# A chunked-attention and gated-MLP kernel: 64-row attention tiles without padding, weight factors made during attention, one gated block taken from PSUM

## The chip, the cores and the metric

The kernel runs on one core of one Trainium2 chip. The metric is the device time of one execution in microseconds, lower is better. A time that is given for a kernel is the median of its runs; a profile shows one execution, whose own time is given beside it.

## The reference

Attention in chunks of 32 tokens, each of which sees 16 tokens to its left, 8 to its right and 8 memory tokens, feeds a gated MLP whose gate mixes the tokens of a sequence:

```python
# B, H, S, D = 4, 8, 768, 64; 8 memory tokens; d_model 512, d_ff 1024
for c in range(S // 32):
    k_full = concat([mem_k, k[l_start:r_end]]); v_full = concat([mem_v, v[l_start:r_end]])
    s = q_c @ k_full.T / sqrt(D)
    a = exp(s - max(s)); a = a / (sum(a) + 1e-9)
    attn[c] = a @ v_full
x = attn as (B, S, 512)
h = relu(x @ w_in); u, v = halves of h
v_n = (v - mean) / sqrt(var + 1e-6)
v_s = einsum('ts,bsd->btd', w_spatial, v_n) + b_spatial
out = (u * v_s) @ w_out
```

## The kernel before

**A recorded order.** Every piece of work is recorded with `op(...)` (line 40): its engine, a guessed duration, what it reads and writes, a rank. `Plan.order` (line 64) plays all pieces through once with those guesses, always taking the piece that can start first and, among equals, the one with the lower rank; the program is written out in that order, so each engine runs its pieces strictly in the planner's sequence. Buffers come from rings (`sizes`, line 188), and a piece can also be held back until a slot of its ring is free. All loads and stores but three go through SyncE's queue (`transfer`, line 255), which never has more than a set number of MB outstanding (`window`, 1.5 MB).

**Attention.** A unit `i` is 128 tokens (four chunks of 32) of all eight heads; there are 24 units, six to a batch. The heads lie in four pairs `t`; in a pair, head `r` takes the partitions `r*64` to `r*64+63`. For the scores, `prep` (line 372, ScalarE) copies the keys of a unit into `kmain`, whose slots are 32 keys and 8 memory keys wide. `kmain` is block-diagonal: it has a column block for each of the two heads, and in the block of one head the other head's 64 partitions are zero. So one matmul with all 128 rows, 32 stationary columns of `q` and 2 x 64 moving columns gives the scores of both heads of a pair for one chunk. The values stand in `vmain` in the same manner. The zeros are written once, at the start (lines 239 to 243), and loads, copies and the spreading of the memory rows (`spread_mem`, `spread_keys`) only touch the other parts.

`burst(i)` (line 392) holds the matmuls on TensorE: 16 for the scores of unit `i` (part "s"), 16 for the product with the values of unit `i-1` (part "a"). For the first units the parts are two pieces of work, later they stand together. The target `sx` is a tile of two PSUM banks: all scores in one, all products in the other. Each of these fp32 matmuls appears in the profile as two records, so a part is 32. `softmax` (VectorE and ScalarE), two transposes (`flip`: `pt` for the probabilities, `xt` for the result) and the split of the result into a high and a low fp32r half (`x`) follow.

**MLP, first half.** `ffn_v` and `ffn_u` (lines 549, 588) multiply `x` and `w_in`, each product in three passes (high by high, low by high, high by low). They fill TensorE between the steps of attention as soon as three units of a half sequence are there. The normalised `v` and the `u` go out to DRAM and come back in the second half. `w_in` and `w_out` arrive as 64-bit floats and are taken apart by `from_f64` (line 813: two passes of ScalarE, two of VectorE, an addition on GpSimd); then `right_hand` (line 866) makes the seven right-hand factors.

**Second half.** `spatial(b)` and `ffn_o(b)` (lines 718, 767) are matrix products by a scheme of seven block products (`product`, line 637): p1 to p7 of sums of quarters. VectorE makes the sums (`sm`, line 651) and the low halves (`op`, line 667), ScalarE the high halves (`op`, line 664). Results of `spatial` are collected by a ScalarE copy (`take`, line 731) and a VectorE addition (`join`, line 737) and multiplied with `u` on GpSimd (`gate`, line 745). The seven factors of `w_spatial` come in three pairs of row blocks (`w_sp_pair`, line 913): two are made during attention into `wsp`, the third waits until attention has ended ("attended") and goes to a tile `wsp_end` in memory that attention has given back. `w_out`'s conversion is ordered behind a factor of that third pair (line 903), its factors behind the last matmul of the MLP's first half.

Of the kernel before, what the change touches and what calls it, by code (L numbers as in the profile page):

```python
# [18 lines left out]
CH = 32  # L19
# [6 lines left out]
class Plan:  # L26
# [13 lines left out]
    def op(self, eng, us, fn, r=(), w=(), rank=0.0, mb=0.0, tail=0.0, after=None, alone=False, drag=1.0):  # L40
# [20 lines left out]
        self.ops.append((eng, us, fn, deps, rank, mb, tail, held, begun, alone, drag))  # L61
        return n

    def order(self):
# [9 lines left out]
        lone = 0.0  # L74
# [7 lines left out]
        while len(out) < len(ops):  # L82
# [21 lines left out]
            _, us, _, _, _, mb, tail, held, _, alone, drag = ops[n]  # L104
# [5 lines left out]
            if alone:  # L110
                lone = t + us
            if mb:
# [30 lines left out]
def tile_chunked_attention_gmlp(  # L143
# [44 lines left out]
    sizes = {"f": 3, "sx": 1, "pt": 2, "xt": 1, "y": 5, "st": 8, "big": 4, "uo": 2, "x": 2, "vm": 3,  # L188
             "q": 2, "k": 2, "kT": 2, "p": 1, "xs": 1, "pT": 1, "vr": 2, "op": 4, "sm": 2, "ug": 6, "ot": 11}
    plan = Plan(sizes, {"f", "y", "st", "big", "ot"}, rate=0.30, landing=2.5, lat=0.06, window=1.5, early=(9.0, 4.0))  # L190
# [21 lines left out]
    wsp = const.tile([P, 7, 2, HU - 1, HT], F32R, name="wsp")  # L212
# [110 lines left out]
    def v_of(i):  # L323
        o = (i % NV) * UC
        return vmain[:, :, :, o:o + UC]

    def load_v(i, seq=True, second="SP"):
        b, c0 = i // UB, (i % UB) * UC
        n = UC
        for r in range(2):  # L330
            v4 = v_of(i)[:, :, r].rearrange("p t c d -> p t (c d)")
# [27 lines left out]
    def spread_mem(i, eng, rank):  # L359
        b, o = i // UB, (i % NV) * UC  # L360
        for r in range(2):
            rows = slice(r * D + CH, r * D + SLOT)

            def spread(rows=rows, r=r):
                to, of = vmain[rows, :, r, o:o + UC], memv[rows, b].unsqueeze(2).broadcast_to([M, T, UC, D])
# [6 lines left out]
    def prep(i, rank):  # L372
        for r in range(2):
            rows = slice(r * D, (r + 1) * D)

            def keys(r=r, rows=rows):
                nc.scalar.copy(kmain[i % NK][rows, :, r, :, 0:CH], k_of(i)[rows].rearrange("p t (c s) -> p t c s", s=CH))  # L377
            n = T * (UC + 1) * CH
            op("ACT", act(n), keys, r=qk_keys(i, "k"),
               w=[("kmain", i % NK, r)], rank=rank)  # L380

    def spread_keys(i, rank):
        b = i // UB

        def spread():
            for r in range(2):
                rows = slice(r * D, (r + 1) * D)
# [4 lines left out]
    def burst(i, rank, split=False):  # L392
# [680 lines left out]
```

## Time and profile before

| what | value |
|---|---|
| time, median of 3 runs | 396.16 us (395.98 to 396.25) |
| profiled execution's own time | 395.85 us |
| HBM read, written in it | 45.49 MB, 18.87 MB |
| packets of the main DMA queue | 46900, 64.25 MB, 53.5% of 16 engines' span |
| busiest groups of GpSimd | `ug<-st,ug` 43.8 us, `vmain<-memv` 23.8 us |

The profile gives times from the start of its span. PE is TensorE (PEld its weight loads), DVE VectorE, ACT ScalarE, POOL GpSimd, SP SyncE. In a group `out<-in xN`, out and in are tile names of the program. In a view by windows, each row is a stretch of the span with the busy time of each engine and the number of its instructions, then the granted clock of TensorE, the share of DMA and GB/s.

### The profile page before, as it was taken

The numbers are of one execution on the slowest core, as the hardware profiler recorded it, in microseconds if no ns is written. First come the engines' busy times: TensorE is split into PE (matmuls) and PEld (weight loads), VectorE is DVE, ScalarE is ACT, GpSimd is POOL, SyncE is SP. The second block draws the span as 40 slices with busy tenths as digits, with TensorE's granted clock in tenths as the row PEclk, the third lists the DMA queues.
The fourth block names the chain that finished last, engine by engine and source line by source line (L and its number), as shares of the span: only waits on it lengthen the run. The fifth ranks groups of instructions, "written<-read, shape, count | busy, mean of one in ns | idle before, by whom it ended". The sixth has DMA issues, their size and how long they took to land.

```text
span 394.1 us, 8707 instructions
## 1 busy us (share of the span) xinstructions
PE 368.4 (93%) x3428; PEld 335.0 (85%) x3428; DVE 281.0 (71%) x465; ACT 210.2 (53%) x368; POOL 157.5 (40%) x161
## 2 busy tenths in 40 slices
PE   1659899999999999999999998899999999999996
PEld 1437688898898988988889898799999999999996
DVE  7975965756856558866575499978956794788594
ACT  4765646575456557464434475438434734473361
POOL 8433762193621177601012968770226033403520
PEclk9999999999999999999999999999999999999999
DMA  8998567676575683786603768403640562040014
GB/s 231 309 232 210 129 202 230 183 251 185 182 219 160 235 221 112 211 223 206 187 29 136 257 237 278 136 25 121 210 153 0 162 233 89 0 175 27 2 40 161
DMA packets 47356, 64.93 MB, mean 165 GB/s; under 512 B 4434, under 2 KB 38866, under 8 KB 47316
## 3 DMA queue, kind: packets, MB, share of 16 engines
q1 hardware_dynamic: 46900, 64.25, 53.5%
q8 instruction: 27, 0.44, 0.5%
q10 hardware_dynamic: 416, 0.13, 0.1%
q14 instruction: 13, 0.11, 0.1%
HBM read 45.49 MB, written 18.87 MB: 163 GB/s over the span
## 4 chain that ended last, share of the span: by engine, by line
PE 80%; DVE 8%; issue 2%; ACT 2%; POOL 1%; ACTq 0%
PE y L689 16%; PE f L689 12%; PE f L528 12%; PE sx L395 11%; PE f L530 11%; PE f L529 11%; PE xt L490 3%; PE pt L475 3%; DVE wout L857 2%; DVE sm L651 2%; DVE op L667 2%; POOL ug L745 1%; DVE st L737 1%; ACT op L664 1%; DVE st L834 0%
## 5 line engine op out<-in xcount | busy, mean ns | idle before, releaser
L745 POOL TENSOR_TENSOR ug<-st,ug 128x384 f32<-128x384 f32 x32 | 43.8, 1380 | 79.6 <-DVE st L737 62.0
L528 PE MATMUL f<-x,win_h 128*128 128x384 f32 x128 | 45.8, 358 | 0.0
L574 POOL TENSOR_TENSOR rstd<-ve,mhalf 128x1 f32<-128x1 f32 x24 | 13.5, 562 | 77.4 <-DVE ve L570 75.7
L664 ACT CAST op<-sm 128x768 fp32r<-128x768 f32 x32 | 26.3, 837 | 32.5 <-DVE sm L651 29.9
L530 PE MATMUL f<-x,win_h 128*128 128x384 f32 x128 | 43.2, 338 | 0.0
L529 PE MATMUL f<-x,win_l 128*128 128x384 f32 x128 | 43.0, 336 | 0.0
L528 PE MATMUL f<-win_h,x 128*128 128x512 f32 x96 | 41.6, 433 | 0.0
L689 PE MATMUL y<-wsp,op 128*128 128x384 f32 x192 | 39.5, 341 | 2.0 <-ACT st L731 1.2
L395 PE MATMUL sx<-kmain,q 128*32 128x128 f32 x768 | 28.5, 294 | 11.3 <-ACT kmain L377 9.3
L377 ACT COPY kmain<-k 64x640 f32<-64x640 f32 x48 | 34.7, 724 | 6.8 <-DMA k<-in_k_dram 4.0
L530 PE MATMUL f<-win_l,x 128*128 128x512 f32 x96 | 38.2, 398 | 0.0
L529 PE MATMUL f<-win_h,x 128*128 128x512 f32 x96 | 38.1, 397 | 0.0
L430 DVE TENSOR_TENSOR xs<-sx,rec 128x512 f32<-128x512 f32 x24 | 16.6, 690 | 29.7 <-PE sx L395 29.7
L667 DVE TENSOR_TENSOR op<-sm,op 128x768 fp32r<-128x768 f32 x32 | 33.6, 1056 | 5.3 <-ACT op L664 4.9
L689 PE MATMUL y<-wout,op 128*128 128x256 f32 x288 | 36.2, 280 | 0.8 <-ACT ot L780 0.7
L395 PEld LDWEIGHTS sx<-kmain,q 128*32 128x32 f32 x768 | 21.5, 117 | 18.2 <-POOL vmain L369 10.1
L689 PEld LDWEIGHTS y<-wsp,op 128*128 128x128 f32 x192 | 33.9, 188 | 3.2 <-ACT st L731 1.9
L689 PEld LDWEIGHTS y<-wout,op 128*128 128x128 f32 x288 | 34.9, 188 | 1.2 <-ACT ot L780 0.9
L369 POOL COPY vmain<-memv 8x1024 f32<-8x1024 f32 x22 | 23.8, 1083 | 17.6 <-PE sx L395 16.2
L689 PE MATMUL f<-wsp,op 128*128 128x384 f32 x144 | 29.4, 339 | 1.5 <-DVE op L667 1.5
L599 ACT ACTIVATE uo<-f 128x384 f32<-128x384 f32 x32 | 15.6, 490 | 26.8 <-PE f L530 17.7
L689 PE MATMUL f<-wout,op 128*128 128x256 f32 x216 | 27.3, 280 | 0.0
(100 smaller groups left out, 833.4 us busy)
## 6 DMA issues: line engine op xcount, KB each, us to landing
vmain<-in_v_dram SPq DMA_DIRECT2D x48, 128.0 KB
vn_far<-st SPq DMA_DIRECT2D x24, 256.0 KB
u_far<-uo SPq DMA_DIRECT2D x32, 192.0 KB
vr<-vn_far SPq DMA_DIRECT2D x8, 768.0 KB
ug<-u_far SPq DMA_DIRECT2D x16, 384.0 KB
q<-in_q_dram SPq DMA_DIRECT2D x11, 512.0 KB
out_dram<-ot SPq DMA_DIRECT2D x36, 128.0 KB
vmain<-in_v_dram SPq DMA_DIRECT2D x47, 96.0 KB
```

What stands on the lines that cost most here:

```text
L369: {"DVE": nc.vector, "POOL": nc.gpsimd}[eng].tensor_copy(to, of)
L377: nc.scalar.copy(kmain[i % NK][rows, :, r, :, 0:CH], k_of(i)[rows].rearrange("p t (c s) -> p t c s", s=CH))
L395: nc.tensor.matmul(o, w_, m, start=True, stop=True, skip_group_check=True)
L430: nc.vector.tensor_tensor(xs, t_["sx", i][:, 1], rec.unsqueeze(3).broadcast_to([P, T, 2, D]), op=ALU.mult)
L528: nc.tensor.matmul(o, lh, rh, start=(j == 0), stop=False)
L529: nc.tensor.matmul(o, ll, rh, start=False, stop=False)
L530: nc.tensor.matmul(o, lh, rl, start=False, stop=(j == len(pairs) - 1))
L599: op("ACT", act(HT), lambda: nc.scalar.activation(alloc("uo", i, [P, HT], F32), t_["f", n], AF.Relu), r=[("f", n)], w=[("uo", i)], rank=rank)
L664: nc.scalar.copy(half(0), of())
L667: nc.vector.tensor_tensor(half(1), of(), half(0).bitcast(F32), op=ALU.subtract)
L689: nc.tensor.matmul(o, x, y, start=first and m == 1 and not (seed and bank != "x"), stop=m == 3 * chunks, skip_group_check=True)
L745: nc.gpsimd.tensor_tensor(g, t_[st(x)], g, op=ALU.mult)
```

## The change

- `kmain` and `vmain` lose the axis of the two heads: head `r` keeps its 64 partitions, and nothing is padded. The zeroing of both goes. Each attention matmul takes 64 rows, 32 stationary columns and 64 moving columns, so there are 32 in a part where there were 16. `sx` now has a bank for each head `r` (scores and products of one head share a bank), and the VectorE steps on it read through both banks.
- `prep` is one copy over 128 partitions where it was two over 64; so is `spread_keys`.
- All three pairs of `w_spatial` factors are made during attention, at units 6, 10 and 14, into a larger `wsp`; `wsp_end` goes. `w_out`'s loads and its conversion from 64 bits no longer wait for a `w_spatial` factor (their rank is 260, the loads' 180); its factors stay behind the MLP's first half.
- Block p4 of `spatial` is multiplied with `u` by VectorE, straight from PSUM; before, ScalarE copied it and GpSimd multiplied it.
- `spatial(1)` and `spatial(2)` put two block products ahead of the `ffn_o` before them in rank, where it was one.
- The planner's guesses change (attention pieces, transposes, some GpSimd pieces; VectorE and GpSimd slow each other), `st` has 9 slots for 8, and the window of outstanding transfers is 1.75 MB for 1.5.

```diff
-            _, us, _, _, _, mb, tail, held, _, alone, drag = ops[n]
+            _, us, _, _, _, mb, tail, held, _, alone, drag, shared = ops[n]
+            beside, pace = {"DVE": (free["POOL"] if shared else 0.0, 1.75), "POOL": (both, 1.4)}.get(e, (0.0, 1.0))
+            if beside > t:
+                us += min((beside - t) * (1 - 1 / pace), us * (pace - 1))
...
-    wsp = const.tile([P, 7, 2, HU - 1, HT], F32R, name="wsp")
+    wsp = const.tile([P, 7, 2, HU, HT], F32R, name="wsp")
...
-    vmain = values.tile([P, T, 2, NV * UC, D], F32, name="vmain")
+    vmain = values.tile([P, T, NV * UC, D], F32, name="vmain")
     NK = sizes["kT"]
-    kmain = [values.tile([P, T, 2, UC + 1, SLOT], F32, name=f"kmain{j}") for j in range(NK)]
+    kmain = [values.tile([P, T, UC + 1, SLOT], F32, name=f"kmain{j}") for j in range(NK)]
     nc.vector.memset(mhalf, -0.5)
-    nc.gpsimd.memset(kmain[0], 0.0)
-    for j in range(NV):
-        nc.vector.memset(vmain[:, :, :, j * UC:(j + 1) * UC], 0.0)
     make_identity(nc, ident)
-    nc.gpsimd.memset(kmain[1], 0.0)
...
     def prep(i, rank):
-        for r in range(2):
-            rows = slice(r * D, (r + 1) * D)
-
-            def keys(r=r, rows=rows):
-                nc.scalar.copy(kmain[i % NK][rows, :, r, :, 0:CH], k_of(i)[rows].rearrange("p t (c s) -> p t c s", s=CH))
...
+        def keys():
+            nc.scalar.copy(kmain[i % NK][:, :, :, 0:CH], k_of(i).rearrange("p t (c s) -> p t c s", s=CH))
...
-                alloc("sx", i, [P, 2, T, 2, D], F32, psum=True)
+                alloc("sx", i, [P, 2, 2, T, D], F32, psum=True)
             sx = t_["sx", i]
-            tiles = [(t, c, slice(c * CH, (c + 1) * CH)) for t in range(T) for c in range(UC)]
+            tiles = [(t, c, r, slice(r * D, (r + 1) * D)) for t in range(T) for c in range(UC) for r in range(2)]
...
-                for t, c, rows in tiles:
-                    mm(sx[rows, 0, t], tq[:, t, rows], kT[:, t, :, c * SLOT:c * SLOT + WIN])
+                for t, c, r, rows in tiles:
+                    mm(sx[c * CH:(c + 1) * CH, r, 0, t], tq[rows, t, c * CH:(c + 1) * CH],
+                       kT[rows, t, c * SLOT:c * SLOT + WIN])
...
-                for t, c, rows in tiles:
-                    mm(sx[rows, 1, t], pT[:, t, rows], vt[:, t, :, c])
+                for t, c, r, rows in tiles:
+                    mm(sx[c * CH:(c + 1) * CH, r, 1, t], pT[rows, t, c * CH:(c + 1) * CH], vt[rows, t, c])
...
             elif name == "p4":
-                take("c21")
-                gate("c21", 1, 0)
+                u = ("ug", (b, 1, 0))
+
+                def go():
+                    g = t_[u][:, p]
+                    nc.vector.tensor_tensor(g, t_[bank], g, op=ALU.mult)
+                op("DVE", dve(HT), go, r=[bank], w=[(*u, p)], rank=rank)
...
-        (zu, ku), (zd, kd) = [from_f64(("wout", d), w_out[d * P:(d + 1) * P], rank, load_rank, True, [("wsp", HU - 1, 3, "h")]) for d in (c + 2, c)]
+        (zu, ku), (zd, kd) = [from_f64(("wout", d), w_out[d * P:(d + 1) * P], 260.0, load_rank, True) for d in (c + 2, c)]
...
-        if i in (UB, UB + 7):
-            w_sp_pair((i - UB) // 7, 10.0 * i + 15)
-        if i == UB + 10:
+        if i - UB in (0, 4, 8):
+            w_sp_pair((0, 4, 8).index(i - UB), 10.0 * i + 15)
+        if i == UB + 11:
             load_bias(10.0 * i)
...
-    w_sp_pair(HU - 1, 205.0)
     for c in range(2):
-        w_out_pair(c, 260.0, 200.0)
+        w_out_pair(c, 260.0, 180.0)
...
-            next(spatials[b])
+            for _ in range((1, 2, 2, 1)[b]):
+                next(spatials[b])
```

How the written-out order moves at three places. The first is TensorE in the middle of attention, a combined burst between matmuls of the MLP (`f<-x,win` and `f<-win,x`); before:

```order
L530 MATMUL f<-x,win_h 128x384
L395 MATMUL sx<-kmain_145,q 32x128 x16
L395 MATMUL sx<-vmain,pT 32x128 x16
L528 MATMUL f<-win_h,x 128x512
L529 MATMUL f<-win_h,x 128x512
L530 MATMUL f<-win_l,x 128x512
```

and after:

```order
L527 MATMUL f<-x,win_h 128x384
L388 MATMUL sx<-kmain_145,q 32x64 x32
L388 MATMUL sx<-vmain,pT 32x64 x32
L525 MATMUL f<-win_h,x 128x512
L526 MATMUL f<-win_h,x 128x512
L527 MATMUL f<-win_l,x 128x512
```

The burst stands in the same place; it has twice the matmuls, each with half the moving columns.

The second is VectorE where the MLP's first half ends and the second half begins (`sm`, `op` and `vr` belong to the first `spatial`, `wout` to the factors of `w_out`, `st<-big,st` to its conversion); before:

```order
L833 TENSOR_SCALAR st<-st 128x512
L834 SCALAR_TENSOR_TENSOR st<-big,st 128x512
L651 TENSOR_TENSOR sm<-sm,vr 128x768
L833 TENSOR_SCALAR st<-st 128x512
L834 SCALAR_TENSOR_TENSOR st<-big,st 128x512
L667 TENSOR_TENSOR op<-sm,op 128x768
L857 TENSOR_TENSOR wout<-big,wout 128x256
L651 TENSOR_TENSOR sm<-vr,sm 128x768
L857 TENSOR_TENSOR wout<-big,wout 128x2x256
```

and after:

```order
L647 TENSOR_TENSOR sm<-vr 128x768
L664 TENSOR_TENSOR op<-vr,op 128x768
L575 TENSOR_SCALAR st<-st,mvar,rstd 128x512
L647 TENSOR_TENSOR sm<-sm,vr 128x768
L664 TENSOR_TENSOR op<-sm,op 128x768 x2
L647 TENSOR_TENSOR sm<-vr 128x768
L858 TENSOR_TENSOR wout<-big,wout 128x256
L858 TENSOR_TENSOR wout<-big,wout 128x2x256
```

The conversion of `w_out` has left this place; it now stands among the last units of attention (`den` and `xs` are steps of a unit):

```order
L455 TENSOR_REDUCE den<-p 128x8
L456 TENSOR_TENSOR den<-den,eps 128x8
L458 RECIPROCAL rec<-den 128x8
L834 TENSOR_SCALAR st<-st 128x512
L835 SCALAR_TENSOR_TENSOR st<-big,st 128x512
L834 TENSOR_SCALAR st<-st 128x512
L835 SCALAR_TENSOR_TENSOR st<-big,st 128x512
L424 TENSOR_TENSOR xs<-sx,rec 128x2x4x64
```

The third is GpSimd at the third pair of `w_spatial` factors (`big` holds the raw rows and sums, `rstd` is the root of `ffn_v`); before, behind the last unit:

```order
L574 TENSOR_TENSOR rstd<-ve,mhalf 128x1 x5
L881 TENSOR_TENSOR big<-big 128x384
L857 TENSOR_TENSOR wsp_end<-big,wsp_end 128x384
L857 TENSOR_TENSOR wsp_end<-big,wsp_end 128x2x384
L881 TENSOR_TENSOR big<-big 128x384 x3
L574 TENSOR_TENSOR rstd<-ve,mhalf 128x1
```

and after, with units still to come (`kmain` and `k` belong to them):

```order
L883 TENSOR_TENSOR big<-big 128x384
L858 TENSOR_TENSOR wsp<-big,wsp 128x384
L883 TENSOR_TENSOR big<-big 128x384
L858 TENSOR_TENSOR wsp<-big,wsp 128x2x384 x2
L571 TENSOR_TENSOR rstd<-ve,mhalf 128x1
L883 TENSOR_TENSOR big<-big 128x384 x2
L308 MEMSET k 128x4x16
L382 COPY kmain_144<-memT 128x4x4x8
```

The same eight pieces of GpSimd stand some units earlier.

More of the change, by code (lines that the diff above doesn't have):

```diff
@@ L111, in order @@
                 lone = t + us
+            if shared:
+                both = t + us
             if mb:
@@ L385, in spread @@
         def spread():
-            for r in range(2):
-                rows = slice(r * D, (r + 1) * D)
-                nc.gpsimd.tensor_copy(kmain[i % NK][rows, :, r, 0:UC, CH:SLOT],
-                                      memT[rows, b].unsqueeze(2).broadcast_to([D, T, UC, M]))
-        op("POOL", 0.6, spread, r=["memT"], w=[("kmem", i % NK)], rank=rank)
+            nc.gpsimd.tensor_copy(kmain[i % NK][:, :, 0:UC, CH:SLOT], memT[:, b].unsqueeze(2).broadcast_to([P, T, UC, M]))
+        op("POOL", 0.3, spread, r=["memT"], w=[("kmem", i % NK)], rank=rank)
     def burst(i, rank, split=False):
@@ L421, in burst @@
                 writes.append(("sx", i, 1))
-                us += 0.7
+                us += 0.75 if "s" in what else 0.5
             op("PE", us, lambda what=what: go(what), r=reads, w=writes, rank=rank, tail=0.25)
@@ L651, in go @@
                 {"DVE": nc.vector, "POOL": nc.gpsimd}[sum_eng].tensor_tensor(a, in0(), in1(), op=o)
-            op(sum_eng, dve(W) if sum_eng == "DVE" else pool_(W), go, r=keys, w=[sm], rank=rank)
+            op(sum_eng, dve(W) if sum_eng == "DVE" else pool_(W), go, r=keys, w=[sm], rank=rank,
+               shared=sum_eng == "DVE")
             return (lambda: t_[sm].rearrange("p (s n) -> p s n", s=chunks)), [sm]
@@ L668, in left @@
             op("ACT", act(W), high, r=keys, w=[(*ok, "h")], rank=rank)
-            op("DVE", dve(W), low, r=[*keys, (*ok, "h")], w=[(*ok, "l")], rank=rank)
+            op("DVE", dve(W), low, r=[*keys, (*ok, "h")], w=[(*ok, "l")], rank=rank, shared=True)
             return half, [(*ok, "h"), (*ok, "l")]
@@ L764, in spatial @@
         return product("s", b, ["p1", "p2", "p6", "p5", "p7", "p4", "p3"], [quarter(0, 0), quarter(0, 1), quarter(1, 0), quarter(1, 1)], HU, 2 * P, 2, HT,
-                lambda i, x, s: w_sp_at(i, x, s), lambda i: [("wsp", s, i) for s in range(HU)], "DVE", True, done)
+                lambda i, x, s: wsp[:, i, x, s], lambda i: [("wsp", s, i) for s in range(HU)], "DVE", True, done)
     def ffn_o(b):
@@ L842, in from_f64 @@
         op("ACT", 0.66, rest, r=[("big", big)], w=[("big", big, "r")], rank=rank)
-        op("POOL", 1.35, add, r=[("big", big, "r"), zk] if home else [("big", big, "r")],
+        op("POOL", 1.6 if home else 1.35, add, r=[("big", big, "r"), zk] if home else [("big", big, "r")],
            w=[("big", big)] if home else [zk], rank=rank)
@@ L858, in split @@
         op("ACT", act(n), high, r=reads, w=[(*w, "h") for w in writes], rank=rank)
-        op(eng, pool_(n) if eng == "POOL" else dve(n), low, r=[*reads, *[(*w, "h") for w in writes]], w=writes, rank=rank)
+        op(eng, pool_(n) if eng == "POOL" else dve(n), low, r=[*reads, *[(*w, "h") for w in writes]], w=writes, rank=rank,
+           shared=eng == "DVE")
     def w_in_part(c, part, rank, load_rank, sub_eng):
@@ L924, in w_sp_pair @@
         (u, ku), (d, kd) = raw
-        right_hand("wsp", s, HT, u, d, ku + end, kd + end, lambda i, x: w_sp_at(i, x, s), rank, "POOL", "POOL")
+        right_hand("wsp", s, HT, u, d, ku, kd, lambda i, x: wsp[:, i, x, s], rank, "POOL", "POOL")
     def load_bias(rank):
```

60 lines of the change are left out of this document (27 added, 33 removed).

## The prediction

> **What bounds the kernel now.** I read the page's totals first, then a view by windows, then the bursts in the timeline, then the chain of waits at both ends of the attention phase.
>
> ```profile
> span 394.1 us, 8707 instructions
> PE 368.4 (93%) x3428; PEld 335.0 (85%) x3428; DVE 281.0 (71%) x465; ACT 210.2 (53%) x368; POOL 157.5 (40%) x161
> ```
>
> TensorE is idle for 394.1 - 368.4 = 25.7 us. The windows say where:
>
> ```profile
> core 0: us, PE busy (x) PEld busy (x) DVE busy (x) ACT busy (x) POOL busy (x), PEclk, DMA share, GB/s
> 0.00:30.00 30.00, 13.99 (x147) 9.94 (x148) 24.01 (x36) 17.94 (x29) 16.06 (x22) 1.00 0.99 258
> 30.00:60.00 30.00, 27.79 (x327) 21.86 (x326) 21.97 (x45) 17.41 (x31) 16.77 (x21) 1.00 0.66 181
> 60.00:206.00 146.00, 146.00 (x1757) 127.06 (x1756) 94.78 (x197) 81.48 (x138) 49.42 (x62) 1.00 0.64 190
> 206.00:234.00 28.00, 28.00 (x178) 25.77 (x177) 17.60 (x32) 14.51 (x25) 16.84 (x15) 1.00 0.57 200
> ...
> 240.00:250.00 10.00, 8.41 (x46) 7.57 (x44) 9.93 (x13) 4.22 (x8) 6.25 (x6) 1.00 0.48 149
> 250.00:260.00 10.00, 8.15 (x44) 7.46 (x44) 9.11 (x9) 5.30 (x10) 8.83 (x6) 1.00 0.41 153
> 260.00:270.00 10.00, 9.34 (x65) 9.13 (x64) 7.64 (x9) 4.33 (x9) 5.46 (x5) 1.00 0.00 0
> 270.00:380.00 110.00, 109.90 (x754) 109.64 (x753) 81.67 (x110) 54.81 (x101) 32.68 (x24) 1.00 0.32 108
> ```
>
> From 60 to 234 us TensorE is never idle, though DMA is busy 64% and VectorE 65% (94.78 of 146). There, what shortens TensorE's own work shortens the kernel, and nothing else does. Around 240 to 270 it lacks 1.59 + 1.85 + 0.66 = 4.1 us while VectorE is full (9.93 and 9.11 of 10). From 270 to 380 it is full again. The first 60 us lose 18.2 us to loads and conversions. So the change has three places: the bursts, the start, the turn from attention to `spatial`.
>
> **The bursts.** One combined burst, between matmuls of the MLP:
>
> ```profile
> 103.50 0.34 PE L530 MATMUL f<-x,win_h 128*128 128x384 f32 x1
> 103.77 1.08 PE L395 MATMUL sx<-kmain,q 128*32 128x128 f32 x32
> 104.67 1.06 PE L395 MATMUL sx<-vmain,pT 128*32 128x128 f32 x32
> 105.66 0.44 PE L528 MATMUL f<-x,win_h 128*128 128x384 f32 x1
> ```
>
> A part of 32 records starts 104.67 - 103.77 = 0.90 us before the next part: 28 ns for a weight load and a matmul. Around a burst there are about 0.3 us of entering and leaving that stay. The chain of waits counts how many parts stand where TensorE is the bound; these are the first and last combined burst (x64, 18 of them) and the first and last single part (x32) behind the start, of which there are 5:
>
> ```profile
> 45.50 1.01 PE sx L395 x32
> ...
> 62.36 1.88 PE sx L395 x64
> ...
> 201.40 1.88 PE sx L395 x64
> ...
> 211.00 1.01 PE sx L395 x32
> ```
>
> That makes 18 x 2 + 5 = 41 of the 48 parts. After the change a part has 64 records (a combined burst x128) with half the moving columns. What does it take? The inside of the burst in fine windows, TensorE and its loads:
>
> ```profile
> core 0: us, PE busy (x) PEld busy (x), PEclk, DMA share, GB/s
> 103.76:103.80 0.04, 0.03 (x4) 0.03 (x4) 1.00 0.85 154
> 103.80:103.90 0.10, 0.10 (x4) 0.10 (x8) 1.00 0.78 184
> 103.90:103.94 0.04, 0.04 (x8) 0.04 (x8) 1.00 0.65 205
> ```
>
> Four matmuls have started within 40 ns; then for 100 ns none does, although four more weight loads are done with their issue; then the next four start together. So the matmuls go in lots of four, one lot per some 110 ns, which 32 records in 0.90 us confirm (8 lots of 112 ns). The rows do not say what closes a lot. If a lot is closed because the four column tiles of 128 x 32 are taken, then eight tiles of 64 x 32 make lots of eight, each with half the columns: 64 records in 8 lots of 56 ns, **0.45 us**. If a lot is four matmuls whatever their tiles, it is 16 lots of 56 ns, **0.90 us** as now. If the sequence of load and matmul keeps its 28 ns, it is 64 x 28 = **1.80 us**. The first end has for it that four starts fit into 40 ns, so issue alone allows eight in some 80 ns; the second has that a lot did not start early though it was loaded. I take the middle of these two, **0.67 us**: eight starts in 80 ns instead of 56 make 64 x 10 = 0.64 us, which is nearest to it. Saving 0.225 us a part, 41 x 0.225 = **9.2 us**; by the ends 18.5, 0 and a loss of 41 x 0.90 = 36.9 us.
>
> [...]
>
> VectorE's steps on `sx` keep their element counts but jump between banks. Nearest rows: the split `x`, which writes in strides, and the contiguous `p`:
>
> ```profile
> L449 DVE TENSOR_TENSOR p<-sx,mx 128x512 f32<-128x512 f32 x24 | 16.5, 689 | 5.4 <-PE sx L395 4.9
> L499 DVE TENSOR_TENSOR x<-xt,x 128x512 fp32r<-128x512 f32 x24 | 16.5, 688 | 9.5 <-ACT x L495 9.3
> ```
>
> Same time, so I cost it at nothing. ScalarE loses half of its key copies, behind a full TensorE:
>
> ```profile
> L377 ACT COPY kmain<-k 64x640 f32<-64x640 f32 x48 | 34.7, 724 | 6.8 <-DMA k<-in_k_dram 4.0 <-PE sx L395 2.2
> ```
>
> 24 x 0.72 = 17.4 us less ScalarE work; GpSimd's key spreading halves too. From 60 us on both are worth nothing while TensorE has no gap. Six loads move up SyncE's queue (two of `w_spatial`, four of `w_out`), and the window grows: with DMA at 0.64 and 0.57 of its time and TensorE full, I take nothing for that, nor for a ninth `st` slot.
>
> **The start.** The chain of waits has key copies ahead of the first and of the third part:
>
> ```profile
> 6.14 1.46 ACT L377 COPY kmain<-k 64x640 f32<-64x640 f32 x2 [3.42 <-DMA k<-in_k_dram]
> 7.70 1.94 PE L395 MATMUL sx<-kmain,q 128*32 128x128 f32 x32 [7.70 <-ACT kmain L377]
> 26.32 0.73 ACT kmain L377
> 27.10 1.94 PE sx L395 x32
> ```
>
> The two copies become one of the same length: 0.73 us at 6.14, and one copy fewer ahead of 26.32, **1.5 us** in all. The zeroing that goes (VectorE, GpSimd) ended before the keys' DMA or beside it, so it gains nothing by itself. Faster parts in the cold start count for nothing here, since loads (DMA 0.99 busy) and conversions set the pace. Ends: 0, if the conversion of `w_in` is what is late in any case, and 4.7 us, if the seven early parts, which at 1.94 us are twice as long, also move their units up at the best end (1.5 + 7 x 0.45); I stay with the two rows.
>
> **The turn.** VectorE in the window 229 to 268 us, GpSimd in 206 to 268 us, by group:
>
> ```profile
> L834 DVE SCALAR_TENSOR_TENSOR st<-big,st 128x512 uint32<-128x512 uint32 x4 | 3.3, 826 | 0.1
> L737 DVE TENSOR_TENSOR st<-f,st 128x384 f32<-128x384 f32 x6 | 3.3, 547 | 0.0
> L833 DVE TENSOR_SCALAR st<-st 128x512 uint32<-128x512 uint32 x4 | 2.8, 695 | 0.0
> L745 POOL TENSOR_TENSOR ug<-st,ug 128x384 f32<-128x384 f32 x8 | 11.1, 1406 | 2.5 <-DVE st L737 2.5
> L857 POOL TENSOR_TENSOR wsp_end<-big,wsp_end 128x768 fp32r<-128x768 f32 (+1 forms) x4 | 7.9, 1984 | 5.4 <-ACT wsp_end L853 5.4
> L881 POOL TENSOR_TENSOR big<-big 128x384 f32<-128x384 f32 x4 | 4.0, 1019 | 0.0
> ```
>
> `w_out`'s conversion leaves VectorE there: 3.3 + 2.8 = 6.1 us. Two gates of p4 come to it, which I price as the join L737 that also reads PSUM: 2 x 0.55 = 1.1 us. Net 5.0 us off a VectorE that is full, against 4.1 us that TensorE waits. Not all of that wait is VectorE's own: from 257 us on the chain runs over GpSimd's gates, of which two leave (2 x 1.41). `spatial(1)`'s second block product (18 matmuls) also stands ahead of `ffn_o(0)` and covers the sums it needs. I take **3.5 us**; the ends are 4.1 us and, if the factors of `w_out` (still there) close the gap again, 0.
>
> Where the work goes: 6.1 us of VectorE into 206 to 234 us or just before, where it has 28 - 17.6 = 10.4 us free; 7.9 + 4.0 = 11.9 us of GpSimd into 60 to 206 us, where it has 146 - 49.4 free. Both are covered by a full TensorE; without that cover they would cost up to 6.1 us.
>
> In the later `spatial`s the p4 block keeps its PSUM bank until VectorE, not ScalarE, has come to it. Behind the gate stand the low halves of the next block product, for which TensorE waits. Price at most 8 x 0.55 = 4.4 us; with VectorE at 81.67 of 110 us there and TensorE full I take nothing.
>
> **The sum**, against the profiled execution's own 395.85 us (span 394.1 and 1.75 around it): 395.85 - 9.2 - 1.5 - 3.5 = 381.65 us. The median of the runs, 396.16, is 0.3 above that execution, so I forecast **382.0 us**.
>
> **The rivals.**
> - *Tiles don't run side by side* (the change doesn't do what it says): lots stay at four, a part stays at 0.90 us. For it: the loaded lot that waited. Only the 1.5 and 3.5 remain: 391.2 us.
> - *Eight side by side*: a part takes 0.45 us. 395.85 - 18.5 - 5.0 = 372.4, with the 0.3 372.7 us. Against it: eight starts must fit into 56 ns where four took most of 40.
> - *Issue becomes the bound* (slower): each load and matmul keeps its 28 ns, since nothing in this trace shows more than four records to sustain a quicker pace; 64 of them take 1.80 us. 395.85 + 36.9 - 5.0 + 0.3 = 428.1 us. It decides from the point at which a part costs 5.0 / 41 = 0.12 us more than 0.90, that is above 16 ns a pair.
> - *Attention gets a new bound*: with TensorE done sooner, VectorE and GpSimd (w_spatial, w_out) are late for some bursts, and TensorE waits as much as it saved: 395 us or a little on either side. Against it: VectorE's 65% would only become 94.78 / (146 - 36 x 0.225), 69%.
>
> **How the numbers follow.** Forecast 50%, no tiles side by side 20%, eight side by side 15%, issue 9%, a new bound 6%. The range 372 to 393 us reaches from the full gain to the case without any in the bursts, with 2 us for the unknown of start and turn, and leaves out the last two cases and a little beyond the full gain. About 0.2% (0.8 us) is what a measurement of this kernel can tell from no change. Faster by more than that: the first three cases and a third of the last, 0.87; the rest of the last splits, so same 0.03 and slower 0.10.
>
> **What would show it.** [...] TensorE's matmul count must be 3428 + 1536. The first burst should start near 7.0 us. From 60 us to the end of the MLP's first half TensorE must stay without gaps; a wait on VectorE or ScalarE there would be the new bound. In the 30 us behind that end, less than 1 us of TensorE's time should be idle, and VectorE's rows of the turn must be without `st<-big`. The forecast is wrong above all if a part is not near 0.67 us: each 0.1 us is 4.1 us of the kernel.

## The result, and the profile after

The kernel after takes **380.83 us** (median of 4 runs, 378.39 to 383.24), the kernel before beside it 396.07 us (394.88 to 396.25): a ratio of 0.9621 [0.9541, 0.9702]. A second set of five runs on another chip gave 382.9 us (381.06 to 383.96) and 0.967 [0.9647, 0.9694]. Ratios leave out executions more than 1.5% above the fastest of their kernel (one of e3, three of e9, one of e10; why they took longer is not known), while the medians below have them, so where the two differ the ratio counts. The profiled execution of the kernel after is the shortest one, 378.39 us; before's is 395.85 us.

The page of the kernel after, totals and the queue that carries instructions; the last line is that queue on the page of before, with its packets, MB and share:

```profile
span 376.2 us, 11734 instructions
PE 355.6 (95%) x4964; PEld 327.8 (87%) x4964; DVE 275.0 (73%) x470; ACT 188.8 (50%) x336; POOL 139.8 (37%) x143
q8 instruction: 39, 0.64, 0.7%
```

```profile
q8 instruction: 27, 0.44, 0.5%
```

TensorE has 1536 more matmul records and yet 12.8 us less busy time (368.4 before). The instruction queue has 12 more packets of some 16 KB, one for each 1536 / 12 = 128 records more. The experiments come back to that row.

The view by windows of the kernel after:

```profile
core 0: us, PE busy (x) PEld busy (x) DVE busy (x) ACT busy (x) POOL busy (x), PEclk, DMA share, GB/s
0.00:30.00 30.00, 14.68 (x320) 10.79 (x320) 20.39 (x37) 15.71 (x27) 13.39 (x18) 0.89 0.97 255
30.00:60.00 30.00, 27.95 (x670) 23.40 (x655) 22.83 (x44) 17.55 (x32) 16.79 (x19) 1.00 0.85 215
60.00:195.00 135.00, 135.00 (x2639) 118.46 (x2639) 93.97 (x195) 72.03 (x126) 59.87 (x68) 1.00 0.71 215
...
230.00:240.00 10.00, 10.00 (x59) 10.00 (x58) 9.02 (x12) 5.02 (x9) 3.37 (x3) 1.00 0.72 243
240.00:250.00 10.00, 10.00 (x60) 10.00 (x59) 7.42 (x10) 3.59 (x6) 4.84 (x4) 1.00 0.00 0
250.00:260.00 10.00, 10.00 (x81) 10.00 (x80) 7.67 (x10) 5.96 (x13) 3.36 (x2) 1.00 0.36 117
260.00:370.00 110.00, 110.00 (x770) 109.80 (x769) 83.82 (x117) 52.43 (x98) 21.57 (x16) 1.00 0.30 102
```

From 60 to 370 us TensorE is never idle, in the turn neither. The 0.89 of the first row is a stretch of 6.8 us at a granted clock of 0.50, from 22.4 us on; e1 shows what such a stretch does. The first matmul of `spatial` shows how much had been gained by then; before and after, from the timeline:

```profile
234.26 0.34 PE L683 MATMUL y<-bias,ones 128*128 128x384 f32 x1
```

```profile
223.35 0.34 PE L680 MATMUL y<-bias,ones 128*128 128x384 f32 x1
```

So 10.9 us come from start and bursts. From there to the start of the last matmul it is 156.24 us before and 149.34 us after: 6.9 us more from the turn and what follows.

The burst at 105.9 us in the timeline, and its first 0.25 us in fine windows (x counts the records that were running, and none had ended yet):

```profile
105.86 0.86 PE L388 MATMUL sx<-kmain,q 64*32 64x64 f32 x64
106.51 0.96 PE L388 MATMUL sx<-vmain,pT 64*32 64x64 f32 x64
107.40 0.45 PE L525 MATMUL f<-x,win_h 128*128 128x384 f32 x1
```

```profile
core 0: us, PE busy (x), PEclk, DMA share, GB/s
105.85:105.90 0.05, 0.05 (x8) 1.00 1.03 369
...
105.95:106.00 0.05, 0.05 (x18) 1.00 1.29 307
...
106.05:106.10 0.05, 0.05 (x32) 1.00 0.72 256
```

Eight records begin within 50 ns and 32 within 0.24 us. The other 32 of the part take 0.65 - 0.24 = 0.41 us: 7.5 ns each at first, 13 ns each later. From burst to next matmul it is 107.40 - 105.86 = 1.54 us, where before it was 105.66 - 103.77 = 1.89.

### The profile page after: what moved, and what is told of

It reads as the page before. It is cut to its first block, busy times and chain, and to the rows that moved or that the text cites. A ratio compares the mean times of both kernels' runs of the same rounds, so it can differ in the third digit from the quotient of the medians.

```text
span 376.2 us, 11734 instructions
## 1 busy us (share of the span) xinstructions
PE 355.6 (95%) x4964; PEld 327.8 (87%) x4964; DVE 275.0 (73%) x470; ACT 188.8 (50%) x336; POOL 139.8 (37%) x143
## 4 chain that ended last, share of the span: by engine, by line
PE 91%; DVE 4%; ACT 2%; DMA 1%; issue 1%; SPq 0%; ACTq 0%; DVEq 0%
PE y L686 22%; PE f L686 17%; PE f L525 13%; PE f L526 12%; PE f L527 12%; PE sx L388 10%; PE xt L487 3%; PE pt L472 3%; DMA k<-in_k_dram 1%; DVE st L835 1%; DVE st L834 1%; DVE mx L441 1%; DVE p L445 0%; PE y L680 0%; PE f L680 0%
## 5 line engine op out<-in xcount | busy, mean ns | idle before, releaser
L742 POOL TENSOR_TENSOR ug<-st,ug 128x384 f32<-128x384 f32 x24 | 33.1, 1392 | 97.7 <-DVE st L734 97.7
L686 PE MATMUL y<-wsp,op 128*128 128x384 f32 x288 | 52.6, 336 | 0.0
L686 PEld LDWEIGHTS y<-wsp,op 128*128 128x128 f32 x288 | 50.1, 188 | 0.0
L686 PE MATMUL f<-wsp,op 128*128 128x384 f32 x216 | 40.1, 336 | 0.0
L686 PEld LDWEIGHTS f<-wsp,op 128*128 128x128 f32 x216 | 37.6, 188 | 0.0
L571 POOL TENSOR_TENSOR rstd<-ve,mhalf 128x1 f32<-128x1 f32 x24 | 14.6, 610 | 52.2 <-DVE ve L567 51.8
L388 PEld LDWEIGHTS sx<-kmain,q 64*32 64x32 f32 x1536 | 17.5, 110 | 17.1 <-POOL vmain L370 9.5
L388 PE MATMUL sx<-kmain,q 64*32 64x64 f32 x1536 | 21.5, 235 | 10.6 <-ACT kmain L375 8.4
L370 POOL COPY vmain<-memv 8x1024 f32<-8x1024 f32 x22 | 23.5, 1075 | 10.2 <-PE sx L388 8.5
## 6 DMA issues: line engine op xcount, KB each, us to landing
ug<-u_far SPq DMA_DIRECT2D x16, 384.0 KB
```

Source lines behind the costliest of these rows:

```text
L370: {"DVE": nc.vector, "POOL": nc.gpsimd}[eng].tensor_copy(to, of)
L388: nc.tensor.matmul(o, w_, m, start=True, stop=True, skip_group_check=True)
L571: nc.gpsimd.tensor_tensor(a, t_["ve", i], mhalf, op=ALU.pow)
L686: nc.tensor.matmul(o, x, y, start=first and m == 1 and not (seed and bank != "x"), stop=m == 3 * chunks, skip_group_check=True)
L742: nc.gpsimd.tensor_tensor(g, t_[st(x)], g, op=ALU.mult)
```

## The experiments

All ran beside the kernel before, whose medians were 395.89 us (first four), 395.41 (next four) and 395.52 (last four).

| experiment | median us | ratio to before [95%] |
|---|---|---|
| e1 the kernel after again | 382.9 | 0.9670 [0.9647, 0.9694] |
| e2 64-row tiles alone | 393.01 | 0.9931 [0.9908, 0.9954] |
| e3 third pair and `w_out` held back | 387.64 | 0.9799 [0.9764, 0.9834] |
| e4 other order of tiles | 380.67 | 0.9609 [0.9581, 0.9638] |
| e5 152 records more, one tile | 391.22 | 0.9886 [0.9866, 0.9906] |
| e6 e2 with the 152 records | 400.52 | 1.0138 [1.0118, 1.0158] |
| e7 planner's numbers of before | 385.26 | 0.9744 [0.9718, 0.9770] |
| e8 p4 block by ScalarE and GpSimd | 381.61 | 0.9663 [0.9629, 0.9698] |
| e9 76 records more, four tiles | 386.83 | 0.9726 [0.9680, 0.9773] |
| e10 e4 with the 76 records | 385.0 | 0.9724 [0.9700, 0.9747] |
| e11 one block product ahead | 380.15 | 0.9626 [0.9594, 0.9658] |
| e12 `w_out` alone held back | 389.19 | 0.9850 [0.9825, 0.9875] |

### The same kernel again (e1)

No edit.

> The changed kernel once more, for its spread: its four times lay at 378.4, 378.9, 382.8 and 383.2 us. If that is two courses of one program, single runs lie near 378.6 or near 383.0 and hardly between, and the profile of one near 383 shows the 4 us in one place. If it is plain scatter, they spread evenly over 378 to 383 and the median is near 381.

382.9 us; its profiled execution took 383.75 us, 5.4 more than the first profile of the same program. Its five times lie between 381.1 and 384.0 us without a gap between two groups, which does not look like two courses; but most of the difference stands in one place. 3.9 us are there in the first single part behind the start (45.70 against 41.82 us), and all of it when `spatial` begins (228.69 against 223.35). The timeline of the burst at 32 us, first in the shorter execution, then in e1; the last bracket is TensorE's idle time and what ended it, where "issue" is nothing that the profile shows:

```profile
32.69 0.78 PE L388 MATMUL sx<-vmain,pT 64*32 64x64 f32 x54
33.75 0.33 PE L388 MATMUL sx<-vmain,pT 64*32 64x64 f32 x10 [0.28 <-issue]
34.01 0.50 PE L525 MATMUL f<-win_h,x 128*128 128x512 f32 x1
```

```profile
31.97 0.77 PE L388 MATMUL sx<-vmain,pT 64*32 64x64 f32 x54
37.26 0.45 PE L388 MATMUL sx<-vmain,pT 64*32 64x64 f32 x10 [4.51 <-issue]
37.63 0.79 PE L525 MATMUL f<-win_h,x 128*128 128x512 f32 x1
```

Both stop behind the 54th of 64 records, for 0.28 and 4.51 us, and no engine or load releases them. e3, e4, e7, e8, e2, e11 and e12 stop behind the same 54th record of that product, for 3.14, 2.95, 2.01, 0.49, 0.55, 0.23 and 0.60 us. In e1 one packet moved on the instruction queue between 34 and 36 us:

```profile
q8 instruction: 1, 0.02, 4.1%
```

4.1% of 16 engines for 2 us is 1.3 us. In the shorter execution such a packet moved between 31 and 32 us instead. So TensorE seems to wait for its own instructions. This was tried with e5, e6, e9 and e10.

The stop has a second price. Behind it the granted clock of e1 is halved for 3.4 us:

```profile
core 0: us, PE busy (x) PEld busy (x) DVE busy (x) ACT busy (x) POOL busy (x), PEclk, DMA share, GB/s
37.27:40.68 3.41, 3.41 (x18) 2.55 (x19) 2.84 (x6) 0.00 (x0) 0.00 (x0) 0.50 0.20 67
```

In it, matmuls of 512 columns start 0.43 us apart, against 0.23 us behind it. (The start of the kernel before has 0.43 us too, from 29.56 to 31.27 us, at a granted clock of 1.00, so the pace alone doesn't tell the clock.) Where TensorE is the bound, 3.4 us at a clock of 0.50 cost 1.7 us, an estimate from the 3.4 us and the 0.50. Not every stop is followed by such a stretch (e9's of 2.0 us at 51.3 us is not), and waits for other engines can be followed by one too (e12).

### The tiles alone (e2)

The kernel before with 64-row matmuls and compact `kmain` and `vmain`; all conversions, the gate and the planner's numbers as before:

```diff
-                for t, c, rows in tiles:
-                    mm(sx[rows, 0, t], tq[:, t, rows], kT[:, t, :, c * SLOT:c * SLOT + WIN])
+                for t, c, r, rows in tiles:
+                    mm(sx[c * CH:(c + 1) * CH, r, 0, t], tq[rows, t, c * CH:(c + 1) * CH],
+                       kT[rows, t, c * SLOT:c * SLOT + WIN])
```

> The kernel before with the 64-row tiles, the compact keys and values and nothing else. Theory: the bursts give 18 x 0.34 + 5 x 0.21 = 7.2 us less about 1 for hitches, whatever else is done, and the turn keeps its idle 4 to 5 us of TensorE: 387 to 390 us, the 1024 matmuls behind the attention start 7 to 10 us earlier than at 234.3. Rival: what TensorE saves in the bursts comes back as waits of the bursts on VectorE or ScalarE while attention runs, and the gain came from the conversions and the planner: 393 us or more, with gaps of TensorE between 60 and 210 us. Second rival: the start's 3.6 us belong to the tiles too (no zeroing, one key copy): 384 to 386.

393.01 us: the 387 to 390 of the theory was missed. The rival's time and its gaps came, but less than half of the idle time is a wait for ScalarE or VectorE. Its profiled execution took 395.0 us. Who waited for whom on TensorE between 60 and 210 us, where before there was no wait at all (us in total, times, longest):

```profile
PE sx L383 <- issue: 3.1, 3, 1.7
PE pt L467 <- ACT p L445: 2.2, 2, 1.3
PE f L521 <- DVE x L491: 0.4, 1, 0.4
```

There are two kinds of wait. Transposes wait for ScalarE's exponential, 2.2 us: TensorE was sooner there and ScalarE was not. And bursts stop by themselves again, 3.1 us. The idle time of the turn stays (56 us from 232 hold 51.71 us of TensorE). In this execution `spatial` begins at 232.79 us, only 1.5 us earlier than before, where the kernel after gains 10.9. Stops took 4.2 us up to there (3.1 in this window), waits for ScalarE and VectorE 2.6, and 3.4 us at a granted clock of 0.50 behind the stop of 1.7 us cost another 1.7 by the estimate above: 8.5 of the 9.4 us that are missing.

### The conversions held back (e3, e12)

e3 puts the third pair of `w_spatial` into a tile of its own behind attention, with `w_out`'s conversion behind it; e12 holds `w_out`'s conversion alone:

```diff
-    wsp = const.tile([P, 7, 2, HU, HT], F32R, name="wsp")
+    wsp = const.tile([P, 7, 2, HU - 1, HT], F32R, name="wsp")
...
+        end = ["attended"] if s == HU - 1 else []
...
+    w_sp_pair(HU - 1, 205.0)
```

```diff
-        (zu, ku), (zd, kd) = [from_f64(("wout", d), w_out[d * P:(d + 1) * P], 260.0, load_rank, True) for d in (c + 2, c)]
+        (zu, ku), (zd, kd) = [from_f64(("wout", d), w_out[d * P:(d + 1) * P], rank, load_rank, True, ["attended"]) for d in (c + 2, c)]
```

> The changed kernel with the third pair of w_spatial factors and w_out's conversion back behind attention, as before; tiles, gate and planner's guesses as changed. Theory: the turn's 5 us come from these: 4 to 6 us above the changed kernel's median, and TensorE idles 4 us or more in the 40 us behind the MLP's first half. Rival: the block of spatial that moved ahead of ffn_o and the gate on VectorE closed the gap: within 1 us of the changed kernel. A matmul of 384 columns in the second half takes 173.5 ns in the changed kernel and 175.7 before; if the second tile wsp_end was the cause, it is back at 175.7.

> The kernel after with w_out's conversion alone held until the last x is written; all three pairs of w_spatial stay in the attention phase. With both held back the turn had 4.66 us of idle time and the time rose by 4.7. Theory: VectorE's conversions of w_out (eight instructions of some 1.1 us and its differences) stand ahead of the first product's operands, so 2 to 4 us of the idle time come back, 384 to 387 us. Rival: the third pair of w_spatial was what the turn waited for; then under 1 us comes back, 381 to 384 us. Beside it: if the matmuls of 384 columns run at 173.5 ns here too and at 175.6 only where the third pair has a tile of its own, that pace goes with the tile and not with w_out.

387.64 and 389.19 us. e3 is 4.7 us above e1, as its theory had it; e12 is above its theory's 384 to 387. TensorE's waits between 215 and 290 us, of e3 and then of e12:

```profile
PE y L687 <- DVE op L665: 4.4, 3, 3.1
```

```profile
PE f L686 <- DVE op L664: 4.5, 1, 4.5
PE y L686 <- DVE op L664: 2.2, 2, 1.3
```

Both wait for VectorE's low halves `op`. What stands ahead of them in e12, on VectorE:

```profile
221.03 0.69 DVE L835 SCALAR_TENSOR_TENSOR st<-big,st 128x512 uint32<-128x512 uint32 x1
...
222.09 1.68 DVE L835 SCALAR_TENSOR_TENSOR st<-big,st 128x512 uint32<-128x512 uint32 x1
223.69 1.61 DVE L664 TENSOR_TENSOR op<-vr,op 128x768 fp32r<-128x768 f32 x1
225.22 3.69 DVE L858 TENSOR_TENSOR wout<-big,wout 128x256 fp32r<-128x256 f32 x3
```

`st<-big` is `w_out` being converted, and `wout<-big` are its factors. `w_out` on VectorE alone is thus enough for the turn's waits, with 6.7 us even more than together with the third pair, whose differences GpSimd makes; why it is more was not tried. From the first matmul of `spatial` to the last matmul e12 takes 158.93 us, 9.6 more than the kernel after: the 6.7 us, and for most of the rest a granted clock of 0.50 from 231.1 to 237.9 us, in which TensorE works for 4.5 us (worth some 2.3).

A second thing showed by the way. The chain of waits has runs of matmuls of 384 columns, before and after:

```profile
321.78 3.18 PE y L689 x18
```

```profile
304.63 3.12 PE y L686 x18
```

18 matmuls take 3.17 to 3.18 us where the third pair has its tile `wsp_end` (before; e3 has 3.15 to 3.18) and 3.12 us where it lies in `wsp` (after; e12 too). At 0.05 us for 18, the 504 such matmuls (288 into `y`, 216 into `f`) give 1.4 us. Which property of the tile does it was not tried.

### The order of the tiles in a burst (e4)

```diff
-            tiles = [(t, c, r, slice(r * D, (r + 1) * D)) for t in range(T) for c in range(UC) for r in range(2)]
+            tiles = [(t, c, r, slice(r * D, (r + 1) * D)) for t in range(T) for r in range(2) for c in range(UC)]
```

> The changed kernel with the order of tiles in a part turned: all four column tiles of head 0, then the four of head 1, where the two heads alternated. Same matmuls, same planner's order. Theory A: what starts together is limited by the row tiles among consecutive matmuls; matmuls of one row tile go in lots of four, so the first half of a part takes 0.45 us in place of 0.24 and a part 0.85 to 0.95: 6 to 10 us slower. Theory B: free tiles alone decide and eight start together in either order; the slower second half of a part is the issue of instructions, 16 to 17 ns for a load and a matmul: a part stays at 0.70 us and the kernel within 1 us.

380.67 us. Most combined bursts take 1.51 us instead of 1.54, and the 18 together 28.1 instead of 28.6, so the order hardly matters. That free tiles and the issue of records set the pace, and not which neighbours follow each other, fits this; it was not shown apart. Most of the 2.2 us under e1 are stops, see the table below.

### Where a stop stands in the instruction stream (e5, e6, e9, e10)

Matmuls with no use, ahead of the warm-up matmuls at 12.4 us, move every later instruction in TensorE's stream. e5 and e6 add 76 matmuls to one tile. They turned out to be two records each, so 152. e9 and e10 add 38, over four tiles:

```diff
+            for j in range(38):
+                rows = slice(j % UC * CH, (j % UC + 1) * CH)
+                nc.tensor.matmul(o[rows, 0:D], ident[0:D, 0:CH], ident[0:D, 0:D], start=True, stop=True, skip_group_check=True)
```

> The kernel after, with 76 more matmuls of 64x64 ahead of the four warm-up matmuls, where TensorE stands idle from 12.4 to 15.4 us. They add some 1.3 us there, inside the idle time, and 152 instructions to TensorE's stream, so that each place of the stream comes 76 matmuls earlier by count. Theory (the code): in three of four profiles of kernels with this start TensorE stops inside the burst at 32 us behind the same 54th of 64 matmuls, 3.0 to 4.5 us, and goes on 1.4 to 1.6 us after a packet of 16 KB of the instruction queue has ended. If the stop is the wait for the next instructions, it leaves that burst: the burst takes 0.8 to 1.2 us, the next single part starts at 41.3 to 42.2 us instead of 43.6 to 45.7, and the time is 377 to 380.5 us. Rival (data): the burst waits for its v or pT, or for a buffer; then the stop stays behind the 54th matmul of that burst with 3 us or more in most executions, and the time stays at 381 to 384.

> The kernel before with the 64-row matmuls alone, and the same 76 matmuls at the start. Without them the profile had stops of 0.5 to 1.6 us inside the bursts at 61.8, 125.0 and 181.5 us (behind 127, 114 and some 115 of 128 matmuls), and 1.3 and 1.0 us ahead of transposes at 66 and 156 us. Theory (the code): the stops are at places of the stream that are 128 matmuls apart, so they leave these matmuls and turn up at others, or not; the bursts at 61.8, 125.0 and 181.5 take 1.40 to 1.55 us, and the time is between 388.5 and 393. Rival (data or buffers): the same bursts stop behind the same matmuls, and the time is 392 to 395.

> The kernel after, with 38 matmuls of 64x64 (76 records) over four tiles ahead of the four warm-up matmuls. The run before this one had put 152 records into one tile, which took 108 ns each and pushed the start back by 11.7 us. Over four tiles they should take some 27 ns each, 2.1 us in all, between 12.4 and 15.4 us where TensorE stands idle; the first matmul of the MLP stays at 24.2 to 25.2 us. Theory (the code): the place in the stream that stood behind the 54th record of the burst at 32 us lies 76 records earlier now, 22 records before that burst begins, and the packet that is due there is asked for during the long matmuls of 24 to 29 us. The burst at 32 us then takes 0.64 to 0.9 us, the next single part starts at 41.0 to 41.8 us, and the time is 377.5 to 381 us, 2 us or more under the 382.9 of the kernel after on the other chip. Rival (the stop only finds another place in the three bursts of 28 to 33 us, or it is a wait for data): a stop of 0.5 to 4.5 us remains there, and the time is 380 to 384.

> The same 76 records, and the bursts in the order of the run that gave 380.67 us (all four column groups of one half of the rows, then of the other). If both gains hold (a burst is 0.03 us shorter in this order, and the stop of 3.0 us in its start goes), 376.5 to 380 us, 0 to 1 us under the run with the code alone moved; if that order's 2.2 us over the kernel after was only the scatter of the stop, the two are equal within 0.5 us.

The times were missed in all four. The places moved, though in e9 to where its rival had them: into another burst close by. e5's matmuls did not take 1.3 us:

```profile
L540 PE MATMUL f<-ident 64*32 64x64 f32 x152 | 16.4, 311 | 0.0
```

That is 108 ns each, one after the other in one tile, which pushed the first MLP matmul from 24.58 to 36.24 us; the time rose by about as much. Its burst has no stop any more (1.04 us up to the next matmul). In e6 the stops of e2 inside the bursts at 61.8, 125.0 and 181.5 us are gone from their successors (1.55, 1.66 and 1.71 us up to the next matmul), and a stop of 2.2 us stands in another burst, behind its 124th record. The waits for ScalarE's exponential stayed ahead of the same transposes (75.8 and 167.9 us), so they are of the other kind.

e9's four tiles took 2.3 us in idle time. 76 records earlier than the 54th of that burst is the 47th record of the burst before it, and there the stop stands:

```profile
32.23 0.71 PE L388 MATMUL sx<-kmain,q 64*32 64x64 f32 x47 [0.23 <-DVE xs L424]
34.83 0.35 PE L388 MATMUL sx<-kmain,q 64*32 64x64 f32 x17 [1.89 <-issue]
```

So a stop belongs to a place in the stream, counted in records, and not to a datum or a buffer. Between 32.0 and 32.1 us an instruction packet begins to move:

```profile
q8 instruction: 1, 0.02, 76.7%
```

76.7% of 16 engines for 0.1 us is 1.2 us, so it ends at 33.3 us, and TensorE goes on 1.5 us later. That TensorE waits for this packet is inferred from the place, the times and the 128 records for each packet; the profile doesn't name its receiver.

All the traces together bear the inference out. The number of packets goes with TensorE's records alone: 27 for 3428, 39 for 4964 and 5040, 40 for 5116, while the instructions of the other engines stay nearly the same or become fewer (VectorE 465 before and 470 after, ScalarE 368 and 336). The fourteen profiled executions have 42 stops put down to "issue". Counted in TensorE's matmul records from the start of the stream, 39 of them stand behind records 348, 474, 728, 981, 1107 and on up to 3644: all within 2 records of 348 and a multiple of 126.75, whatever the program. The same 39 end 1.2 to 1.7 us behind the end of an instruction packet. The other three, at record 755 (e2, e7) and 907 (e6), fit neither and stay unexplained.

A combined burst of the kernel after is 128 records. By the 128 records for each packet that the two pages give, it uses up a packet's worth in 1.54 us, an estimate.

Moving the place was no cure. e9 has stops at other places, from the view of waits:

```profile
PE sx L388 <- issue: 5.3, 4, 2.0
PE f L525 <- issue: 1.5, 1, 1.5
PE f L527 <- issue: 0.7, 1, 0.7
```

The sum of these "issue" waits accounts for most of the scatter between programs that differ little. Profiled executions:

| kernel | time us | waits by "issue" us | difference |
|---|---|---|---|
| after | 378.39 | 0.3 | 378.1 |
| e8 | 379.48 | 1.5 | 378.0 |
| e11 | 379.62 | 1.5 | 378.1 |
| e4 | 380.98 | 3.0 | 378.0 |
| e1 | 383.75 | 5.4 | 378.4 |
| e10 | 385.0 | 5.3 | 379.7 |
| e9 | 386.25 | 7.5 | 378.8 |
| e7 | 386.35 | 4.4 | 382.0 |
| e12 | 388.21 | 2.0 | 386.3 |
| e3 | 388.34 | 4.2 | 384.1 |
| e5 | 389.42 | 0.3 | 389.1 |
| e2 | 395.0 | 4.2 | 390.8 |
| before | 395.85 | 0 | 395.85 |
| e6 | 402.27 | 3.4 | 398.9 |

That some agree to 0.1 us is partly chance. e10's 1.7 us over the others are 3.4 us at a granted clock of 0.50 (49.6 to 53.0 us). e1 and e4 have such a stretch at 37 us, but lack a wait of 1.5 us for VectorE at 39 us that the kernel after, e8 and e11 have. The scatter lies ahead of `spatial`: from its first matmul to the last of all, the kernel after, e1, e5, e9, e10 and e11 each take 149.33 or 149.34 us (e4 takes 150.81 and e8 150.13; less their stops, both are about as much sooner when `spatial` begins).

Why a packet comes in time in one execution of the same program and 3 us late in another stays open.

### The planner's numbers (e7)

The kernel after with the guesses of before, the window of 1.5 MB and 8 `st` slots:

```diff
-            beside, pace = {"DVE": (free["POOL"] if shared else 0.0, 1.75), "POOL": (both, 1.4)}.get(e, (0.0, 1.0))
-            if beside > t:
-                us += min((beside - t) * (1 - 1 / pace), us * (pace - 1))
...
-            us = 0.35
+            us = 0.4
```

> The kernel after with the planner's numbers of before (costs, no slowdown of VectorE and GpSimd beside each other, the window of loads 1.5 MB, 8 buffers of st). Everything computed is the same, only the order of the instructions and the pace of the loads differ. Theory (the order counts): the matmuls alone gained 2.9 us where bursts and start were to give 7 and more, because the order of before lets TensorE stop in the attention phase; then this one takes 385 to 389 us, with 3 us or more of TensorE's idle time between 60 and 210 us. Rival (the order is worth nothing by itself, the turn's conversions and the bursts are): 380 to 384 us, and under 1 us of idle time between 60 and 210 us.

385.26 us, as the theory had it: TensorE idles 3.4 us between 60 and 210 us, part of it on the exponential (1.3 us) as in e2. Without stops it is 382.0 against 378.1, so the new order and pacing of loads are worth some 3.9 us, 0.8 of it behind the first matmul of `spatial` (150.14 against 149.34 us). The guesses, the window and the ring were not told apart.

### The gate and the order of the turn (e8, e11)

```diff
-                op("DVE", dve(HT), go, r=[bank], w=[(*u, p)], rank=rank)
+                take("c21")
+                gate("c21", 1, 0)
```

```diff
-            for _ in range((1, 2, 2, 1)[b]):
+            for _ in range(1):
```

> The kernel after, with the block of the sixth product again copied by ScalarE and gated by GpSimd. The prediction gave the block itself no time of its own in the end. Theory: 0 to +0.7 us, 381 to 384 us, with no idle time of TensorE over 0.3 us behind the first product of the turn. Rival (the block on VectorE frees the bank or GpSimd in the turn): a stop of 0.5 us or more comes back between 223 and 280 us, and the time is 384 or more.

> The kernel after with one block product, not two, ahead of the loop in the two middle rounds of the turn's order. Theory: the turn's waits are gone because of the earlier conversions, so this costs 0 to 0.7 us (381 to 384 us), with under 0.5 us of TensorE's idle time between 220 and 290 us. Rival: the order covers a wait of the turn or of a later round, and TensorE stands 0.8 us or more somewhere between 220 and 376 us.

381.61 and 380.15 us, with no wait of TensorE between 215 and 290 us in either. Less their stops both stand at 378.0 to 378.1, as the kernel after does. From the first matmul of `spatial` to the last, e11 takes the same 149.34 us, so the second product ahead is worth nothing. e8 takes 150.13, with one wait more, at 361.7 us:

```profile
PE y L686 <- DVE op L664: 0.6, 1, 0.6
```

So the gate on VectorE may be worth up to 0.8 us there, as e8's theory allowed; the medians are too wide to tell. In the turn itself neither part does anything.

## Why the prediction came out, step by step

The time and the mechanism of the forecast held; every term of its sum was off. That 382.0 us came so close to the median of 380.83 was in part luck: the three terms together gained 2.5 us more than forecast, while the median lies 2.4 us above the shortest execution, from which the terms are measured, where the forecast had 0.3. Stops that the prediction did not have are the likely cause of that.

- **The bursts, 9.2 us: the step was mis-sized, 6.2 us measured.** A part by itself came as foreseen: a single part takes 0.79 us in the chain instead of 1.01, 0.22 saved where 0.225 stood.

```profile
41.89 0.79 PE sx L388 x53
```

  But combined bursts save 1.89 - 1.54 = 0.35 us and not 0.45, and some are longer: the 18 take 28.6 us up to the next matmul, 1.59 each, where they took 33.8, which saves 5.2 us, and the five singles 1.0. The prediction's 10 ns a record came as 7.5 ns for the first 32 and 13 ns for the rest, whose mean is 10.2: its size for a part was right, but not as an even pace.
- **The rival by issue** (28 ns a pair, 428 us) did not come. It was to decide above 16 ns a pair; 128 records in 1.54 us are 12 ns.
- **The start, 1.5 us: too small, 3.6 us measured** in the first profile (45.50 to 41.89 us in the chain for the first single part). The key copy gave 7.70 - 7.14 = 0.56 us. Most of the rest came from the written-out order of VectorE: the first unit's `xs` starts at 20.78 us where it was 23.67, ahead of work that it stood behind (read from the trace, not tried apart). With the planner's numbers of before it starts at 21.69 (e2) and 21.79 us (e7), and e2 has its first single part at 42.15, so the tiles with their fewer copies and zeroings brought most of this, not the new numbers. The prediction had looked at ScalarE only. In e1 a stop of 4.51 us took all of it back.
- **The turn, 3.5 us: too small, 6.9 us measured.** All of TensorE's idle time behind the start of `spatial` (4.1 us in 234 to 290 us, 0.3 later) went, and some 1.4 us came by the pace of 384-column matmuls, which the prediction didn't have. Some 1 us is not assigned. That VectorE and `w_out` held the turn is shown by e12; the gate and the second product ahead, which the prediction counted in, did nothing in the turn (e8, e11).
- **What was put at nothing** was not nothing: the planner's numbers (some 3.9 us, which lie inside the terms above: without them part of those is lost again). Without them the rival "attention gets a new bound" would partly have come: in e2 and e7 transposes wait for the exponential.
- **What the prediction lacked** is, by the inference above, the supply of instructions. It counted 1536 more records as work of TensorE and not as code that must arrive. The stops take 0.3 to 5.4 us in the two profiles of the kernel after, with a granted clock of 0.50 for 3.4 us behind the longest, and the spread of its runs, 378.4 to 384.0, has become wider than that of before, 394.5 to 396.4.
- Sum: 6.2 + 3.6 + 6.9 = 16.7 of the 17.5 us between the two profiled executions.

Of the signs that the prediction named, the record count (4964), the first burst at 7.14 us, no gap from 60 us on, and no `st<-big` among VectorE's rows between 223 and 262 us came out; the part's 0.67 us came as 0.65 for the first of a pair.

No version beat the kernel after by more than the stops scatter: e11 with 380.15 and e4 with 380.67 us are within it.

## What to carry to other kernels

Splitting a matmul into tiles that run side by side paid less here than the number of tiles promised: a part went from 0.90 to 0.65 us, where twice the tiles with half the columns were to give 0.45 by the prediction's best end. So ask for the time of one part in a trace, and count the instructions as well as the work: here a burst issues 128 records in 1.54 us, one packet of instructions moved for each 128 records more, and TensorE stopped for up to 4.5 us at places about that far apart. When the busy engine becomes faster, the order written for the old durations is part of the change (some 3.9 us in e7); try the change with the old order too. Idle time that nothing in the profile ends, at the same places of the instruction stream in every program (39 of 42 stops here), pointed to the supply of code. Taking it off each time showed most of what an edit did: five executions between 378.39 and 383.75 us come to 378.0 to 378.4 us. Look at the granted clock behind each stop as well: in e1 it was 0.50 for 3.4 us, an estimated 1.7 us more.

## What had not been expected of the hardware

- In the thirteen profiled executions with 64-row matmuls TensorE stops 42 times, for 0.2 to 4.5 us, where nothing in the profile ends the stop. 39 of the 42 stand at fixed places of its instruction stream and end 1.2 to 1.7 us after a packet of the instruction queue. The profile of the kernel before has no such wait.
- A granted clock of 0.50 for 3.4 us follows some stops and waits (e1, e2, e10; 6.8 us in e12). In the stretch of 0.50 at the start of the kernel after (22.4 to 29.2 us), matmuls of 512 columns start 0.43 us apart, at 1.00 from 34.35 us on 0.23.
- Records into one and the same 64 x 32 tile follow each other every 108 ns at the start of the kernel (e5), over four tiles every 30 ns (2.3 us for 76, e9).
- Matmuls of 384 columns ran at 3.12 us for 18 instead of 3.18, depending on whether a part of their factors had a tile of its own.
